# Three chained layers on one core: small layer-norm products inside attention's bursts, four PSUM buffers for the gated layer's first V tiles, output weights split later

## The chip, the core and the metric

The kernel runs on one core of a Trainium2 chip. The metric is the time of the whole program on the device in microseconds, the median of several runs. [...]

## What is computed

Attention over 8 heads in a window of 128 with a linear bias, then a two-matrix layer with a norm in front (the "first layer" below, 512 to 2048 to 512), then a gated layer with a mixing matrix over the 576 positions. Batch 4, model width 512, all in float32.

```python
attn = softmax(scale * q @ k.T + bias, masked to 0 <= rel < 128) @ v
x    = attn as (4, 576, 512)
xn   = (x - mean) / sqrt(var + 1e-6) * g_ln
x    = x + relu(xn @ w_ch1) @ w_ch2
h    = gelu(x @ w_in);  u, v = halves of h
v_n  = norm(v) * g_ln
v_s  = einsum('ts,bsd->btd', w_sg, v_n) + b_sg
out  = x + (u * v_s) @ w_out
```

## The kernel before

Matrix products of float32 accuracy are made of three products of rounded parts: a high part and a low part of each factor (names ending in h and l), without low times low. Splitting is work for the other engines: ScalarE writes the high part, GpSimd (POOL) or VectorE (DVE) the rest. The weight matrices come as 64-bit floats and are first turned to 32 bits by integer operations on VectorE (class Split64, lines 81, 83, 85 and 88), between two ScalarE operations (76 and 92); GpSimd then makes the low part (93).

Phase 1 holds attention and the first layer. Its order is made by a planner (class Sched): each generator yields operations with an engine, a planned duration, a priority, tokens it needs and buffers it takes; the planner always issues what can start first, and the program keeps that order on every engine. Positions are handled in nine groups g of 256 columns (two per batch, and group 8 for the last 64 positions of all batches). The first layer runs as a stream of pieces: m1 (line 785, into PSUM tile ps_h) and m2 (line 796, into PSUM tile acc), each piece 24 matmuls of 256 columns. From run KB = 13 on, attention's TensorE work comes in bursts between such pieces (function burst): scores of the next run (454, or 440 for the last 64 positions), value products of the run before (622, into PSUM tile o), transposes of this one (582, tps). PACE and BB set how early attention's units are due against the stream.

Each group's norm (functions norm, center, spread) needs three small products on TensorE: the mean (644 or 653), the sum of squares (701) and the spread of the reciprocal deviation over all partitions (711). Each is a planner operation of its own and takes one of the two ps_h buffers. For groups 3 to 8 GpSimd first adds the parts, so that one product is enough. The reciprocal deviation is applied only when a group's last m2 is evacuated (735, 739).

At the end of attention (end_attention) PSUM and SBUF space is released, and the generators flow (one per weight block) load and split the gated layer's weights: V half and U half of w_in (wv, wu), the first batch's x (x2), the mixing matrix (ws) and the output weights (wo, four blocks). Two V tiles of the gated layer (early_v) are planned around the last m2 piece, each 12 matmuls of 512 columns (line 1037) into one of two PSUM buffers ps_v.

Phase 2 (Phase2.run) is written in program order with chunks: v_tile (V: product, GELU, norm, split), u_chunk (U: 24 matmuls of 288 columns, GELU), vs_chunk (SG: mixing product of 28 matmuls, gate, split into gh and gl) and out_chunk (O). A V tile's GELU is Square and Tanh on ScalarE (1069, 1071) with VectorE between and behind (1070, 1074); then statistics (1088 to 1090), a power on GpSimd (1091), the norm (1094) and a split (1028, 1029). The parts of the fifth V tile are called vt. play() issues a chunk's matmuls, then one further step of each chunk that is pending, then some ticks; a tick loads and splits weights or the next batch's x. first_tail (971) splits the last 64 columns of the first batch's x2, which come from group 8 of the first layer; every U chunk reads them.

```python
# before, phase 2, first batch
play(V(0)[:2])
self.first_tail(x8)
...
play([V(0)[2], V(0)[3], U(0)[0], V(0)[4]] + U(0)[1:], 2)
self.need("ws")
```

Of the kernel before, what the change touches and what calls it, by code (L numbers as in the profile page):

```python
# [20 lines left out]
G = 2 * B + 1  # L21
# [24 lines left out]
LQ = 1, 0, 3, 2, 4, 8  # L46
EPRI = (-1, 9)

# [10 lines left out]
KB = 13  # L59
BB = 11, 6  # L60

# [160 lines left out]
def phase1(tc, nc, a, x2d, cst, p2):  # L222
# [361 lines left out]
    def burst(s):  # L584
        n = s.n
        after = runs[n + 1] if n + 1 < len(runs) else None
        nd = [("nm", e.un) for e in s.units] + [("bl", e.un - 2) for e in s.units if e.un - 2 < s.units[0].un]
        nd += [("R", n - 1), "cst", "unf"] + ([("A1", n)] if n == KB else [])
        sl = [("o", 1, ("ev", n - 1))]
        if after:  # L590
            nd += [("lq", n + 1), ("lk", n + 1)]
            sl.append(("s", 1, ("cp", n + 1)))
        dur = 300 + 140 * len(s.units) + (400 if runs[n - 1].tail else 820 if runs[n - 1].i0 else 600)
        if after:
            dur += 420 if after.tail else 850 if after.i0 else 600
# [6 lines left out]
        for z in [("A1", n + 1), ("C", n - 1)] + [("T", e.un) for e in s.units]:  # L602
            sched.done[z] = sched.free["PE"] + HOPP
# [27 lines left out]
    def gain(xh, xl, xc, p):  # L631
        act.activation(out=xh[:, p], in_=xc[:, p], func=ACTF.Copy, scale=g1[:, p:p + 1])
        dve.scalar_tensor_tensor(out=xl[:, p], in0=xc[:, p], scalar=g1[:, p:p + 1], in1=xh[:, p].bitcast(F32),
                                 op0=ALU.mult, op1=ALU.subtract)

    def norm(g):
        evs = [("ev", s.n) for s in runs if s.x() == g]
        pri = start[g] - LBACK[g == 8]
        last_m1 = ("m1", *[z for z in stream if z[0] == g][-1], 1)
        if g < NF:  # L640
            yield Op("PE", 1720, pri, need=evs, slots=[("h", 2, ("xc", g))])
            ps = ps_h.tile([128, 2, 256], F32, tag="h", name="ps_ln")
# [38 lines left out]
    def spread(g, xc, pri):  # L681
        pri += LQ[3]
        yield Op("ACT", 1040, pri, slots=[("ls", 2, ("var", g)), ("ls", 2, ("sq2", g))], token=("sq", g))
        sq = [ln_tile("sq") for z in range(2)]
# [3 lines left out]
        if g >= NF:  # L688
            yield Op("POOL", 1260, pri, token=("sq2", g))
            t = sq[0]  # L690
            pool.tensor_tensor(out=t, in0=sq[0], in1=sq[1], op=ALU.add)
            yield Op("POOL", 687, pri)
            pool.tensor_tensor(out=t[:, 0], in0=t[:, 0], in1=t[:, 1], op=ALU.add)
            parts = parts[:1]
        yield Op("PE", 230 * len(parts), pri + LQ[4], slots=[("h", 2, ("ve", g))], token=("var", g))
        if g < NF:
            sched.done["sq2", g] = sched.free["PE"] + HOP
        ps = ps_h.tile([128, 2, 256], F32, tag="h", name="ps_ln")
        for z in range(2):
            for x, t in enumerate(parts):  # L700
                pe.matmul(ps[:, 0, z:z + 1], t[:, 128 * z:128 * z + 128], ones[:, 0:1], start=x == 0,  # L701
                          stop=x + 1 == len(parts))
        yield Op("DVE", 70, pri + LQ[4], token=("ve", g), slots=[("vb", 2, ("rs0", g))])
# [3 lines left out]
        pool.tensor_tensor(out=v, in0=v, in1=mh.to_broadcast([128, 2]), op=ALU.pow)  # L707
        yield Op("PE", 430, pri + LQ[5], slots=[("h", 2, ("rstd", g))], token=("rs0", g))
        ps = ps_h.tile([128, 2, 256], F32, tag="h", name="ps_r")
        for z in range(2):  # L710
            pe.matmul(ps[:, 0, 128 * z:128 * z + 128], v[:, z:z + 1].to_broadcast([128, 128]), ident, start=True,
                      stop=True)
        yield Op("ACT", 275, pri + LQ[5], slots=[("rb", 3, ("x2", g))], token=("rstd", g))
# [191 lines left out]
class Phase2:  # L905
# [124 lines left out]

    def v_products(self, i):
# [9 lines left out]
    def early_v(self, i, pri):  # L1041

        yield Op("PE", 2560, pri, need=[("sc2", n) for n in range(4)] + [("st2", 8)])
        self.early[0, i] = self.v_products(i)

    def run(self, x8, left):
# [240 lines left out]
```

## Time and profile before

| | |
|---|---|
| median of 3 runs | 754.61 us (753.49 to 755.19) |
| profiled execution | 752.81 us, span 750.8 us |
| TensorE (PE) busy | 736.4 us, 98% of the span |
| VectorE, ScalarE, GpSimd busy | 60%, 41%, 33% |
| granted TensorE clock, mean | 0.995 |
| phase 1's last m2 matmul | about 533.4 us after the span's start |

PE's busy time is that of overlapping pipelined matmuls, so its share says that it was never long idle, not that it ran at its peak. The time between the starts of neighbouring rows tells how long a matmul held the engine. Times in rows are microseconds from the span's start.

### The profile page before, as it was taken

How to read it: one execution, taken by the hardware profiler on the slowest of the kernel's cores; microseconds unless marked ns; L12 is line 12 of the kernel's file. 1: busy time of each engine (PE TensorE's matmuls, PEld its weight loads, DVE VectorE, ACT ScalarE, POOL GpSimd, SP SyncE). 2: the span in 40 equal slices, each digit the busy share in tenths (PEclk: the TensorE clock that was granted, in tenths of full speed). 3: DMA queues.
4: the chain of work that ended last, by engine and by line, in shares of the span. 5: the costliest groups of instructions: out<-in, count | busy, mean ns of one | idle time of the engine just before them, and what ended most of it. 6: DMA issues, size and time to landing. Idle time of an engine off the chain costs nothing.

```text
span 750.8 us, 15850 instructions
## 1 busy us (share of the span) xinstructions
PE 736.4 (98%) x6270; PEld 685.9 (91%) x6270; DVE 448.3 (60%) x1149; ACT 308.5 (41%) x795; POOL 245.8 (33%) x307
## 2 busy tenths in 40 slices
PE   7999999999999999999999999999899999999998
PEld 3669899999999999999999999999799999999997
DVE  6899889896643453453343438434966746647632
ACT  5896755544323323433323424233453334243410
POOL 2533432333313212222212423026356307327220
PEclk9999999999999999999999999999999999999999
DMA  8654631331121020021122234304500050160002
GB/s 296 220 176 117 190 106 34 92 106 51 56 89 52 25 69 26 27 85 29 28 66 58 71 90 131 124 30 139 183 24 2 31 173 0 48 206 0 1 33 94
DMA packets 51625, 63.41 MB, mean 84 GB/s; under 512 B 10336, under 2 KB 38880, under 8 KB 51552
## 3 DMA queue, kind: packets, MB, share of 16 engines
q1 hardware_dynamic: 51552, 62.41, 26.5%
q8 instruction: 49, 0.80, 0.4%
q14 instruction: 24, 0.20, 0.1%
HBM read 52.96 MB, written 9.44 MB: 83 GB/s over the span
## 4 chain that ended last, share of the span: by engine, by line
PE 93%; DVE 2%; DMA 1%; ACT 1%; POOL 1%; issue 1%; SPq 0%; DVEq 0%; POOLq 0%; ACTq 0%
PE ps_h L785 26%; PE acc L796 25%; PE ps_s L1130 8%; PE ps_u L1113 7%; PE ps_o L1158 7%; PE ps_v L1037 6%; PE o L622 5%; PE tps L582 3%; PE s L454 3%; PE ps_ln L701 1%; DMA st<-in_w 1%; PE ps_ln L644 1%; DMA st<-in_wo 1%; PE ps_w L356 1%; PE s L440 1%
## 5 line engine op out<-in xcount | busy, mean ns | idle before, releaser
L796 PE MATMUL acc<-hh,w2h 128*128 128x256 f32 x576 | 163.6, 284 | 0.0
L785 PE MATMUL ps_h<-xh,w1h 128*128 128x256 f32 x576 | 163.0, 283 | 0.0
L785 PE MATMUL ps_h<-xl,w1h 128*128 128x256 f32 x576 | 160.2, 278 | 0.0
L785 PE MATMUL ps_h<-xh,w1l 128*128 128x256 f32 x576 | 160.1, 278 | 0.0
L796 PE MATMUL acc<-hl,w2h 128*128 128x256 f32 x576 | 160.1, 278 | 0.0
L796 PE MATMUL acc<-hh,w2l 128*128 128x256 f32 x576 | 160.0, 278 | 0.0
L726 DVE SCALAR_TENSOR_TENSOR hl<-ps_h,hh 128x512 fp32r<-128x512 f32 x72 | 49.7, 690 | 127.3 <-ACT hh L724 127.0
L785 PEld LDWEIGHTS ps_h<-xh,w1h 128*128 128x128 f32 x576 | 108.6, 188 | 1.0 <-issue 0.9
L796 PEld LDWEIGHTS acc<-hh,w2h 128*128 128x128 f32 x576 | 108.7, 189 | 0.7 <-DVE sc L85 0.3
L796 PEld LDWEIGHTS acc<-hl,w2h 128*128 128x128 f32 x576 | 108.4, 188 | 0.2
L785 PEld LDWEIGHTS ps_h<-xl,w1h 128*128 128x128 f32 x576 | 108.4, 188 | 0.1
L785 PEld LDWEIGHTS ps_h<-xh,w1l 128*128 128x128 f32 x576 | 108.3, 188 | 0.0
L796 PEld LDWEIGHTS acc<-hh,w2l 128*128 128x128 f32 x576 | 108.3, 188 | 0.0
L724 ACT ACTIVATE hh<-ps_h 128x512 fp32r<-128x512 f32 x72 | 42.8, 595 | 138.8 <-PE ps_h L785 138.8
L463 POOL TENSOR_SCALAR_AFFINE_SELECT m<-m 128x256 f32<-128x256 f32 x100 | 44.7, 452 | 143.7 <-ACT m L543 141.6
L505 ACT ACTIVATE t<-t,sm 128x128 f32<-128x128 f32 x144 | 56.1, 394 | 14.6 <-DVE sm L499 14.6
L513 POOL TENSOR_TENSOR t<-t,sm 128x256 f32<-128x256 f32 x52 | 32.9, 633 | 42.4 <-DVE sm L509 34.9
L76 ACT ACTIVATE sc<-st 128x512 f32<-128x512 f32 (+1 forms) x52 | 30.9, 599 | 24.6 <-DMA st<-in_w 6.7
L1029 POOL TENSOR_TENSOR gl<-gt,gh 128x576 fp32r<-128x576 f32 x16 | 22.9, 1429 | 53.0 <-ACT gh L1028 53.0
L1071 ACT ACTIVATE ge<-ge 128x512 f32<-128x512 f32 (+1 forms) x34 | 22.4, 657 | 34.9 <-DVE ge L1070 34.9
L85 DVE SCALAR_TENSOR_TENSOR sc<-st,sc 128x512 int32<-128x512 int32 (+1 forms) x52 | 35.9, 692 | 0.3
L622 PE MATMUL o<-m,rv 128*64 128x128 f32 (+3 forms) x416 | 34.7, 296 | 0.3 <-POOL m L463 0.3
(163 smaller groups left out, 1530.5 us busy)
## 6 DMA issues: line engine op xcount, KB each, us to landing
st<-in_w SPq DMA_DIRECT2D x24, 512.0 KB, 4.2
x2d<-x SPq DMA_DIRECT2D x18, 256.0 KB, 2.0
out<-xr SPq DMA_DIRECT2D x15, 288.0 KB, 2.1
st<-in_w SPq DMA_DIRECT2D x16, 256.0 KB, 2.6
st<-in_wi SPq DMA_DIRECT2D x8, 512.0 KB, 3.9
st<-x2d SPq DMA_DIRECT2D x8, 512.0 KB, 5.1
xr<-x2d SPq DMA_DIRECT2D x8, 512.0 KB, 6.3
rq<-in_q SPq DMA_DIRECT2D x28, 128.0 KB, 3.2
```

Of the source, the lines that this page charges most:

```text
L85: dve.scalar_tensor_tensor(out=xi, in0=self.wh, scalar=-0x40000000, in1=xi, op0=ALU.bitwise_and, op1=ALU.bitwise_or)
L463: pool.affine_select(out=out, in_=in_, pattern=pat, compare_op=ALU.is_ge, fill=0.0, base=-1 if up else 0, channel_multiplier=1 if up else -1)
L505: act.activation(out=t[:, h], in_=t[:, h], func=ACTF.Exp, bias=st[:, h:h + 1], scale=-1.0, accum_out=sums[:, h, 0:1])
L622: pe.matmul(s.O[64 * h:64 * h + 64, oc:oc + w], v, s.M[m][0:k, h, mc:mc + w], start=x == 0, stop=x == len(mm) - 1, skip_group_check=True)
L724: act.activation(out=h, in_=ps, func=ACTF.Relu)
L726: dve.scalar_tensor_tensor(out=l, in0=ps, scalar=0.0, in1=h.bitcast(F32), op0=ALU.max, op1=ALU.subtract)
L785: pe.matmul(ps[:, half], w[:, kc, f], m[:, kc], start=kc == 0 and x == 0, stop=kc == 3 and x == 2)
L796: pe.matmul(accs[half][:, d], w[:, f, ds], m[:, k], start=fi and d == 0 and k == 0 and x == 0, stop=la and k == 1 and x == 2, skip_group_c ...
L1037: self.nc.tensor.matmul(ps, xs[s][:, kc, c0:c0 + 128], self.wv[m][:, kc], start=kc == 0 and x == 0, stop=kc == 3 and x == 2)
L1113: pe.matmul(ps[:, z, 0:288], wu[s][:, kc, ds], self.x[m][:, kc, 288 * z:288 * z + 288], start=kc == 0 and x == 0, stop=kc == 3 and x == 2)
L1130: pe.matmul(ps[:, z, 0:288], l, r[:, 288 * z:288 * z + 288], start=n == 0, stop=n == len(mm) - 1)
L1158: pe.matmul(ps[:, z, 0:288], wo[s][:, kc, ds], gated[b][m][:, kc, 288 * z:288 * z + 288], start=n == 0, stop=n == 11)
```

## The change

It has three parts.

1. For groups 3 to 7 the three small products are no longer planner operations of their own. They are put on a list (riders), and the next burst whose needs are met issues them between its value products and its transposes. Their results go to the second half of attention's PSUM tile o (ob[:, 256:512]), not to a ps_h buffer. GpSimd's last addition goes to a buffer of its own (rd). BB's first number moves attention two units ahead.
2. A PSUM pool ps_e with two buffers is opened at the end of attention beside ps_v. Four V tiles are planned early, one ahead of the last m2 piece and three behind it; V tiles 0 and 1 use ps_e. The pool ps_u of phase 2 is opened only after these four tiles have been played, without ticks, and first_tail comes after them. The order after that is U, U, V tile 4, U, U.
3. The output weights (wo) are not split by flow; they remain queued for the ticks of phase 2.

```diff
-EPRI = (-1, 9)
+EPRI = (-1, 9, 10, 11)
-BB = 11, 6
+BB = 13, 6
@@ burst
         values(runs[n - 1])
+        ride = [r for r in riders if all(sched.done.get(z, 1e9) <= sched.now for z in r[0])]
+        for r in ride:
+            riders.remove(r)
+            r[1]()
+            sched.free["PE"] += r[2]
         for e in s.units:
             transposed(e)
@@ new functions
+    def products(g, fn, dur, pri, free, token):
+
+        if g < NF or g == G - 1:
+            yield Op("PE", dur, pri, slots=[("h", 2, free)], token=token)
+            ps = ps_h.tile([128, 2, 256], F32, tag="h", name="ps_ln")
+            fn(ps)
+            return ps
+        ps = ob[:, 256:512].rearrange("p (o c) -> p o c", o=1)
+        yield Op(None, 0, pri, token=("ride", *token))
+        riders.append(((("ride", *token), ("rstd", g - 1)), lambda: fn(ps), dur, token))
+        yield Op(None, 0, pri, need=[token])
+        return ps
+
+    def last_sum(g, t, token, pri):
+
+        y = t[:, 0]
+        yield Op("POOL", 687, pri, slots=[] if g == G - 1 else [("rd", 1, token)], token=("rd", *token))
+        if g < G - 1:
+            y = P["st"].tile([128, 256], F32, tag="rd", name="rd", bufs=1)
+        pool.tensor_tensor(out=y, in0=t[:, 0], in1=t[:, 1], op=ALU.add)
+        return y
@@ norm (spread is changed alike for its two products)
-            yield Op("PE", 427, pri + LQ[1], slots=[("h", 2, ("xc", g))], token=("mean", g))
-            ps = ps_h.tile([128, 2, 256], F32, tag="h", name="ps_ln")
-            pe.matmul(ps[:, 0], ones, t[:, 0], start=True, stop=True)
+            y = yield from last_sum(g, t, ("mean", g), pri)
+            parts = [y]
+
+        def mean(ps):
+            for x, y in enumerate(parts):
+                pe.matmul(ps[:, 0], ones, y, start=x == 0, stop=x + 1 == len(parts), skip_group_check=True)
+
+        ps = yield from products(g, mean, 430 * len(parts), pri + LQ[1] * (g >= NF), ("xc", g), ("mean", g))
@@ end_attention
+        p2.ps_e = tc.alloc_tile_pool(name="ps_e", bufs=2, space=PSUM, side="right", reuse_waits="tile")
-        for n, j in enumerate(list(p2.queue)):
+        for n, j in enumerate(z for z in list(p2.queue) if z.name != "wo"):
             sched.spawn(p2.flow(sched, j, n), sched.now)
-        for i in range(2):
+        for i in range(4):
             sched.spawn(p2.early_v(i, when[2, stream[-1]] + EPRI[i]), sched.now)
@@ v_products
-        ps = self.ps_v.tile([128, DG], F32, tag="v", name="ps_v")
+        ps = (self.ps_e if b == 0 and i < 2 else self.ps_v).tile([128, DG], F32, tag="v", name="ps_v")
@@ Phase2.run
-        play(V(0)[:2])
+        play(V(0)[:4], 0)
+        self.ps_e.release()
+        ps_u = tc.alloc_tile_pool(name="ps_u", bufs=3, space=PSUM, reuse_waits="tile")
         self.first_tail(x8)
...
-        play([V(0)[2], V(0)[3], U(0)[0], V(0)[4]] + U(0)[1:], 2)
+        play(U(0)[:2] + V(0)[4:] + U(0)[2:], 2)
```

TensorE, the sum of squares of group 3 in the first layer. Before, in the middle of an m1 piece:

```order
L785 MATMUL ps_h_2934<-xh_1475,w1h3_2039 128x256
L785 MATMUL ps_h_2934<-xl_1476,w1h3_2039 128x256
L785 MATMUL ps_h_2934<-xh_1475,w1l3_2040 128x256
L701 MATMUL ps_ln_2953<-ones_73,sq_2857 128x1 x2
L785 MATMUL ps_h_2934<-xh_1475,w1h3_2039 128x256
L785 MATMUL ps_h_2934<-xl_1476,w1h3_2039 128x256
```

In the change (line numbers shift; 818 is m1, 627 the value products, 728 the squares):

```order
L818 MATMUL ps_h_3060<-xh_2807,w1l0_95 128x256
L454 MATMUL s_150<-rk_2531,rq_2526 64x64 x2
L454 MATMUL s_150<-rk_2531,rq_2526 64x128 x2
L454 MATMUL s_150<-rk_2531,rq_2526 64x192 x4
L627 MATMUL o_146<-m_2749,rv_2294 64x256 x2
L627 MATMUL o_146<-m_2752,rv_2294 64x128 x2
L728 MATMUL o_146<-ones_73,rd_2844 128x1 x2
L582 MATMUL tps_142<-ident_71,t_2760 128x128 x2
L582 MATMUL tps_142<-ident_71,t_2803 128x128 x2
L818 MATMUL ps_h_3060<-xh_2807,w1h0_94 128x256
```

The two products left the m1 piece for a burst that was there anyway; the same holds for the other 14.

ScalarE at the start of the gated layer (ge is the GELU's tile: Square reads ps_v, Tanh reads ge; x2h of x and xth of x are first_tail). Before:

```order
L1069 ACTIVATE ge_7106<-ps_v_7014 128x512
L1071 ACTIVATE ge_7106<-ge_7106 128x512
L1069 ACTIVATE ge_7113<-ps_v_7065 128x512
L1071 ACTIVATE ge_7113<-ge_7113 128x512
L92 ACTIVATE woh_6935<-sc_7028 128x512
L1028 ACTIVATE x2h_6665<-x_5432 128x4x64
L1028 ACTIVATE xth_6937<-x_5432 128x512
L1028 ACTIVATE vnh_7095<-vg_7107 128x512
```

In the change:

```order
L1105 ACTIVATE ge_7073<-ge_7073 128x512
L1063 ACTIVATE vnh_7059<-vg_7068 128x512
L1103 ACTIVATE ge_7098<-ps_v_7085 128x512
L1105 ACTIVATE ge_7098<-ge_7098 128x512
L1063 ACTIVATE vnh_7059<-vg_7074 128x512
L1103 ACTIVATE ge_7126<-ps_v_7113 128x512
L1105 ACTIVATE ge_7126<-ge_7126 128x512
L1063 ACTIVATE x2h_6666<-x_5325 128x4x64
L1063 ACTIVATE xth_6934<-x_5325 128x512
```

The split of the last columns stood behind two V tiles' Tanh and now stands behind four.

ScalarE in the mixing stage of batch 0 (x2h of st is the split of batch 1's x). Before:

```order
L1071 ACTIVATE ge_7353<-ge_7353 128x576
L1028 ACTIVATE gh_7358<-gt_7389 128x576
L1028 ACTIVATE x2h_6665<-st_7393 128x4x256
L1028 ACTIVATE gh_7358<-gt_7426 128x576
L1028 ACTIVATE x2h_6665<-st_7395 128x4x256
```

In the change, where L1168 and L1171 on VectorE make gt:

```order
L92 ACTIVATE woh_6932<-sc_7263 128x512
L76 ACTIVATE sc_7349<-st_7238 128x512
L92 ACTIVATE woh_6932<-sc_7306 128x512
L1063 ACTIVATE gh_7351<-gt_7382 128x576
L92 ACTIVATE woh_6932<-sc_7349 128x512
L1063 ACTIVATE x2h_6666<-st_7389 128x4x256
L1063 ACTIVATE gh_7351<-gt_7425 128x576
```

The split of batch 1's x now stands behind the fourth output-weight block, whose last VectorE operation stands behind the gate of the second SG chunk:

```order
L1168 SCALAR_TENSOR_TENSOR gt_7425<-ps_s_7396,g2_6798,bb_6797 128x576
L1171 TENSOR_TENSOR gt_7425<-gt_7425,u_7158 128x576
L88 SCALAR_TENSOR_TENSOR sc_7349<-st_7238,sc_7349 128x512
```

Before, no output-weight operation stood in this stage on VectorE.

## Rows read from the trace of the kernel before

**Rows 1.** The page's part 4, the chain that ended last: share of the span by engine.
```profile
PE 93%; DVE 2%; DMA 1%; ACT 1%; POOL 1%; issue 1%; SPq 0%; DVEq 0%; POOLq 0%; ACTq 0%
```

**Rows 2.** TensorE's timeline behind group 3's sum of squares: start, us, instruction.
```profile
200.92 0.36 PE L785 MATMUL ps_h<-xh,w1h 128*128 128x256 f32 x1
201.12 0.28 PE L785 MATMUL ps_h<-xl,w1h 128*128 128x256 f32 x1
```

**Rows 3.** The chain in order of time, two pieces of the stream: start, us, what.
```profile
196.47 2.83 PE acc L796 x24
...
226.87 2.72 PE ps_h L785 x24
```

**Rows 4.** TensorE's timeline, first matmuls of V tiles 1 and 2, U, V tile 4.
```profile
533.50 0.39 PE L1037 MATMUL ps_v<-wvh,x2h 128*128 128x512 f32 x1
...
539.68 0.50 PE L1037 MATMUL ps_v<-wvh,x2h 128*128 128x512 f32 x1 [3.25 <-DVE vg L1074]
...
546.89 0.42 PE L1113 MATMUL ps_u<-x2h,wuh 128*128 128x288 f32 x2
...
550.08 0.40 PE L1037 MATMUL ps_v<-wvh,xth 128*128 128x512 f32 x1
```

**Rows 5.** Windows: us, busy PE PEld DVE ACT POOL, granted clock, DMA share, GB/s.
```profile
540.40:544.00 3.60, 3.60 (x11) 2.79 (x10) 3.19 (x8) 2.50 (x5) 1.94 (x3) 0.53 1.10 389
```

**Rows 6.** The chain in order of time, four SG chunks and two V tiles.
```profile
562.63 14.93 PE ps_s L1130 x112
577.56 5.45 PE ps_v L1037 x24
```

**Rows 7.** VectorE's timeline: last evacuations (L735), GELU and statistics of V tile 1.
```profile
533.54 0.68 DVE L735 TENSOR_TENSOR et<-acc,rstd 128x512 f32<-128x512 f32 x1
...
534.87 0.69 DVE L735 TENSOR_TENSOR et<-acc,rstd 128x512 f32<-128x512 f32 x1
...
540.68 0.68 DVE L1070 SCALAR_TENSOR_TENSOR ge<-ge,ps_v 128x512 f32<-128x512 f32 x1
...
543.72 0.16 DVE L1090 TENSOR_SCALAR ba<-ba 128x1 f32<-128x1 f32 x1
```

**Rows 8.** ScalarE's timeline: Tanh of V tile 1, output weights, first_tail.
```profile
541.39 0.63 ACT L1071 ACTIVATE ge<-ge 128x512 f32<-128x512 f32 x1 [2.22 <-DVE ge L1070]
541.92 0.61 ACT L92 ACTIVATE woh<-sc 128x512 fp32r<-128x512 f32 x1
542.45 0.40 ACT L1028 ACTIVATE x2h<-x 128x256 fp32r<-128x256 f32 x1
```

**Rows 9.** GpSimd's timeline: output weights, first_tail, vt, batch 1's x.
```profile
528.02 1.30 POOL L93 TENSOR_TENSOR wol<-sc,woh 128x512 fp32r<-128x512 f32 x1 [3.64 <-ACT woh L92]
...
543.86 0.74 POOL L1029 TENSOR_TENSOR x2l<-x,x2h 128x256 fp32r<-128x256 f32 x1
...
560.88 2.65 POOL L1029 TENSOR_TENSOR vt<-vg,vt 64x512 fp32r<-64x512 f32 x2 [1.33 <-ACT vt L1028]
...
570.42 2.38 POOL L1029 TENSOR_TENSOR x2l<-st,x2h 128x1024 fp32r<-128x1024 f32 x1
```

**Rows 10.** VectorE's timeline: output weights (L83, L85), U's GELU, gates (L1134, L1137).
```profile
524.97 0.43 DVE L83 TENSOR_SCALAR sc<-sc 128x512 int32<-128x512 int32 x1
525.44 0.69 DVE L85 SCALAR_TENSOR_TENSOR sc<-st,sc 128x512 int32<-128x512 int32 x1
...
528.37 1.49 DVE L85 SCALAR_TENSOR_TENSOR sc<-st,sc 128x512 int32<-128x512 int32 x1
...
552.99 0.74 DVE L1070 SCALAR_TENSOR_TENSOR ge<-ge,ps_u 128x576 f32<-128x576 f32 x1
...
566.52 0.81 DVE L1134 SCALAR_TENSOR_TENSOR gt<-ps_s,g,bb 128x576 f32<-128x576 f32 x1
567.37 0.76 DVE L1137 TENSOR_TENSOR gt<-gt,u 128x576 f32<-128x576 f32 x1
...
570.99 2.44 DVE L1137 TENSOR_TENSOR gt<-gt,u 128x576 f32<-128x576 f32 x1
```

More of the change, by code (lines that the diff above doesn't have):

```diff
@@ L599, in burst @@
         values(runs[n - 1])
+        ride = [r for r in riders if all(sched.done.get(z, 1e9) <= sched.now for z in r[0])]
[3 more added lines that the diff above has]
+            sched.free["PE"] += r[2]
         for e in s.units:
             transposed(e)
-        for z in [("A1", n + 1), ("C", n - 1)] + [("T", e.un) for e in s.units]:
+        for z in [r[3] for r in ride] + [("A1", n + 1), ("C", n - 1)] + [("T", e.un) for e in s.units]:
             sched.done[z] = sched.free["PE"] + HOPP
@@ L634, in gain @@
                                  op0=ALU.mult, op1=ALU.subtract)
+    riders = []
+    def products(g, fn, dur, pri, free, token):
[16 more added lines that the diff above has]
+        return y
     def norm(g):
@@ L640, in norm @@
         if g < NF:
-            yield Op("PE", 1720, pri, need=evs, slots=[("h", 2, ("xc", g))])
-            ps = ps_h.tile([128, 2, 256], F32, tag="h", name="ps_ln")
-            for p in range(4):
-                pe.matmul(ps[:, 0], ones, xt[g][:, p], start=p == 0, stop=p == 3)
+            yield Op(None, 0, pri, need=evs)
+            parts = [xt[g][:, p] for p in range(4)]
         else:
-            yield Op("POOL", 1260, pri, need=evs, slots=[("ls", 2, ("mean", g))])
+            yield Op("POOL", 1260, pri, need=evs, slots=[("ls", 2, ("mean", g) if g == G - 1 else ("rd", "mean", g))])
             t = ln_tile("sum")
             pool.tensor_tensor(out=t, in0=xt[g][:, 0:2], in1=xt[g][:, 2:4], op=ALU.add)
-            yield Op("POOL", 687, pri)
-            pool.tensor_tensor(out=t[:, 0], in0=t[:, 0], in1=t[:, 1], op=ALU.add)
-            yield Op("PE", 427, pri + LQ[1], slots=[("h", 2, ("xc", g))], token=("mean", g))
-            ps = ps_h.tile([128, 2, 256], F32, tag="h", name="ps_ln")
-            pe.matmul(ps[:, 0], ones, t[:, 0], start=True, stop=True)
+            y = yield from last_sum(g, t, ("mean", g), pri)
[4 more added lines that the diff above has]
+        ps = yield from products(g, mean, 430 * len(parts), pri + LQ[1] * (g >= NF), ("xc", g), ("mean", g))
         yield Op("DVE", 1210, pri + LQ[1], need=["al2"], slots=[("xcb", 1, ("xhl", g))], token=("xc", g))
@@ L691, in spread, with squares @@
             pool.tensor_tensor(out=t, in0=sq[0], in1=sq[1], op=ALU.add)
[L692 to L695, printed above, removed]
+            parts[:] = [(yield from last_sum(g, t, ("var", g), pri))]
+        def squares(ps):
+            for z in range(2):
+                for x, t in enumerate(parts):
+                    pe.matmul(ps[:, 0, z:z + 1], t[:, 128 * z:128 * z + 128], ones[:, 0:1], start=x == 0,
+                              stop=x + 1 == len(parts), skip_group_check=True)
+        ps = yield from products(g, squares, 230 * len(parts), pri + LQ[4], ("ve", g), ("var", g))
         if g < NF:
             sched.done["sq2", g] = sched.free["PE"] + HOP
[L698 to L702, printed above, removed]
         yield Op("DVE", 70, pri + LQ[4], token=("ve", g), slots=[("vb", 2, ("rs0", g))])
@@ L707, in spread, with spread_out @@
         pool.tensor_tensor(out=v, in0=v, in1=mh.to_broadcast([128, 2]), op=ALU.pow)
[L708 to L712, printed above, removed]
+        def spread_out(ps):
+            for z in range(2):
+                pe.matmul(ps[:, 0, 128 * z:128 * z + 128], v[:, z:z + 1].to_broadcast([128, 128]), ident, start=True,
+                          stop=True, skip_group_check=True)
+        ps = yield from products(g, spread_out, 430, pri + LQ[5], ("rstd", g), ("rs0", g))
         yield Op("ACT", 275, pri + LQ[5], slots=[("rb", 3, ("x2", g))], token=("rstd", g))
@@ L843, in end_attention @@
     def end_attention():
-        yield Op(None, 0, 0, need=[("ev", s.n) for s in runs] + [("w", n) for n in range(40)], token="attention")
+        yield Op(None, 0, 0, need=[("ev", s.n) for s in runs] + [("w", n) for n in range(40)] + [("rstd", G - 2)],
+                 token="attention")
         for p in (P["st"], raw, ap2, ps_s, ps_o, ps_t):
@@ L1078, in v_tile @@
         def v_tile(b, i):
-            ps = self.early.pop((b, i)) if (b, i) in self.early else self.v_products(i)
+            ps = self.early.pop((b, i)) if (b, i) in self.early else self.v_products(b, i)
             first, last = gelu2(ps, [DG])
```

10 lines of the change are left out of this document (5 added, 5 removed).

## The prediction

> **What bounds the kernel now.** I read the chain of waits first: 93% of the span is TensorE work [rows 1], so a change counts only where it shortens TensorE's own stream or makes TensorE wait. Then TensorE's timeline, for the two places that the change edits.
>
> In the first layer TensorE never waits: its rows follow each other without an idle mark. What can be won there is friction. After a solitary norm product the first matmul holds TensorE for 0.20 us, 200.92 to 201.12 [rows 2]; an ordinary one holds it 0.113 us, 2.72 over 24 [rows 3]. There are also two paces: some pieces of 24 run in 2.72 us, others in 2.83 [rows 3], or 4.6 ns per matmul. Going through the timeline break by break, the slow pace always follows a mean or a squares product; after bursts of six value products it is nearly always fast, after bursts of four it is either.
>
> At the start of the gated layer stands the one long wait. V tile 1 starts at 533.50 and should hand over some 2.73 us later (24 V matmuls take 5.45 [rows 6]), at 536.23; V tile 2 starts at 539.68, after 3.25 us of idle ended by VectorE's GELU of tile 0 freeing a PSUM buffer [rows 4]. [...] So this place costs 3.4 us of waiting and 1.76 us of slow clock.
>
> **Part 1, small products in bursts.** Three products of each of five norms, 15 in all, move behind the value products of a burst. They are the same products, so their own time moves along and I count it as zero. Removed are 15 returns to the stream at 0.20 - 0.113 = 0.09 us [rows 2, 3]: -1.35 us. A burst pays its own return once, as now. Bounds: 0 (the rider pays the same inside the burst) to -2.7 (entering cost as much as leaving). I take -1.35, the end that a row shows.
>
> [...]
>
> The pace: after solitary products of these norms I count eleven slow stretches with 432 matmuls, the first at 189.8 and the last at 431.1 us, so 432 x 4.6 ns = 2.0 us; after bursts another 1.6 us. In the change each such stretch hangs on a burst. If half of them turn fast: -1.0 us. Bounds: all 1920 matmuls of these five blocks slow, 8.8 against 3.6 us now, is +5.2; all fast is -3.6.
>
> The longer latency of a norm (mean, squares and spread now wait a burst each) costs nothing: the gain is applied only when a block ends, and BB starts attention two units earlier. If that cover failed, m1 of the next block would wait for xh and xl.
>
> **Part 2, four PSUM buffers.** The wait at 536.23 goes: V tiles 1 to 3 run from 533.50 to 533.50 + 3 x 2.73 = 541.7. What is late next? The first U product needs the last 64 columns of x2, which first_tail splits, and ScalarE's queue now has that split behind the Tanh of V tile 3. On VectorE the last evacuation can start once the first half of acc is complete, about 532.4 (before it started at 533.54 [rows 7], held up by output-weight splitting). Four operations follow; two take 534.87 - 533.54 = 1.33 us [rows 7], so the GELU of V tile 0 starts at 532.4 + 2.66 = 535.05. One V tile occupies VectorE from the GELU at 540.68 to past 543.72 [rows 7], 3.1 us with the hand-over. Tile 3's GELU: 535.05 + 3 x 3.1 = 544.4. Its Tanh follows 0.71 later (540.68 to 541.39), the next ScalarE instruction 0.53 after that, and x2h takes 0.40 [rows 7, 8]: 546.05. GpSimd's x2l takes 0.74 [rows 9]: 546.85. The fourth matmul of U needs it. So TensorE idles from 541.7 to about 546.8 but for a few matmuls, longer than today. U's remaining 21 of 24 matmuls take 2.8 us (3.19 from 546.89 to 550.08 [rows 4]) and the slow clock again costs 1.76: U ends at 551.4 instead of 550.08. The same five chunks are then done, so this part costs **+1.3 us**, not -5. Bounds: -0.5 if the clock is not lowered this time, +2.5 if VectorE's pitch is 0.4 us longer per tile. Even with VectorE free, tile 3 ends at 541.7 and its GELU, Tanh and x2l still follow, so the gap cannot close.
>
> **Part 3, output weights split later.** Today all four splits start beside the last work of the first layer. Now they enter VectorE, ScalarE and GpSimd between the U and SG chunks. One costs VectorE two operations of 0.43 and two of 0.69, then ScalarE 0.61 (woh) and GpSimd 1.30 (wol) [rows 8 to 10]. The third VectorE operation of the next split waits while GpSimd runs: L85 took 1.49 instead of 0.69 just as wol ran at 528.02 [rows 9, 10]. Following the queues from U's end at 551.4 (U 3.19, V 2.73, SG 3.73 = 14.93/4 [rows 6]):
> - U 1 ends 554.6, V tile 4 557.35, U 2 560.55, U 3 563.75. V tile 4's GELU starts about 558.2; behind it stand three operations of split 1, GELU and statistics, U 2's GELU (0.74), the last of split 1 (to 563.6). Then woh to 564.2, wol to 565.5, the blocked operation of split 2 to 566.2, V tile 4's norm to 566.7. ScalarE and GpSimd make vt: half of 2.65 [rows 9] plus a ScalarE operation like woh, 568.7. SG 0 needs vt for its last four of 28 matmuls, at 563.75 + 3.2 = 566.95: **wait 1.75**.
> - SG 0 then ends at 569.2, SG 1 at 573.0. VectorE has U 3's GELU, splits 2 and 3 and gate 0 (0.81 and 0.76 [rows 10]) before gate 1, which starts about 578 instead of 573. Split 4's last operation stands behind gate 1, ScalarE's woh behind that, and batch 1's x2h behind that: 581.7. GpSimd's x2l (2.38 [rows 9]) is done at 584.4, or a gate product later. TensorE is through with SG 3 at 580.6 and needs x2h at once and x2l two matmuls later: **wait 3.3 to 4.9**.
> Sum 5.0 to 6.7; with 0.2 for a U buffer that comes free late I take **+6.0**. Bounds: 0 (the backlog is covered; today x2l is ready at 572.8, 4.7 us before V(1) starts [rows 6, 9]) to +8.2 (every gate product takes the 2.44 us that one took while GpSimd ran [rows 10]).
>
> A gap of some 4 us before V(1) should lower the clock again, as after 3.25 us today: **+1.76** [rows 4, 5], bounds 0 and 1.76.
>
> **Sum.** The profiled execution took 752.81 us, 1.80 below the median of the runs, 754.61. -1.35 - 1.0 + 1.3 + 6.0 + 1.76 = +6.7: 759.5 on that execution, **761.3 us** on the median.
>
> **Rivals.**
> 1. Not slower: the output splits find room in the U and SG stage, so x2l of batch 1 is complete before SG 3 ends (about 579). Part 3 and the second slow clock are then 0: 754.61 - 1.35 - 1.0 + 1.3 = 753.6. For it: TensorE has no wait in this stage today, and x2l has 4.7 us to spare. Against it: the split of batch 1 stands behind the fourth output split in two queues, which order alone fixes. It decides at a VectorE backlog under some 2 us at gate 1. With all bursts fast as well (-3.6): 751.0.
> 2. Breaks save nothing: behind the riders TensorE needs the same 0.09 us each that it needs today behind a solitary product, and all else stays: 761.3 + 1.35 = 762.7. For it: the riders keep full-array shape among half-array matmuls. Against it: the stream gets 15 returns fewer. [...]
> 3. Riders leave TensorE at the slow pace after every burst: 761.3 + 1.0 + 5.2 = 767.5. For it: every mean and squares product is followed by the slow pace today. Against it: in a burst the transposes come last.
> 4. The wait is removed as meant and nothing takes its place: 754.61 - 5.2 - 2.35 = 747.1 with part 3 hidden. The queue order of part 2 excludes it; I give it 0.02.
>
> **Chances.** A difference under 0.2% (1.5 us) is what a measurement of this kernel cannot tell from none. Forecast 0.65, rival 2 0.10, rival 3 0.05, rival 1 at 753.6 0.12 and with fast bursts 0.06, rival 4 0.02. Slower by over 0.2%: 0.65 + 0.10 + 0.05 = 0.80; same 0.12; faster 0.08. The forecast's own bounds, 756 to 766, hold rival 2; reaching down to 754.5 takes in half of rival 1: 754.5 to 766.
>
> **What would show it.** Right: V tiles 1 to 3 without a wait; then idle of some 4 to 5 us before U with ScalarE's x2h and GpSimd's x2l as releasers and a granted clock near 0.5 behind it; waits on vt in SG 0 and on x2h and x2l of batch 1 before V(1). Part 1 is right if stretches of the first layer lose the 0.20 us returns and its end comes about 2 us earlier. Wrong: U following V tile 3 within 2 us, or V(1) following SG 3 at once.

## The result and the profile after

The changed kernel takes 764.3 us (763.89 to 765.63, 4 runs) against 754.73 us before: a ratio of 1.0132, interval 1.0115 to 1.0150. The forecast was 761.3 in a range of 754.5 to 766.0. Direction and range held; the size, +6.7, came out as +9.6.

The profiled execution took 763.89 us, its span is 762.1. The chain of waits, which was 93% TensorE [rows 1], in the page of the changed kernel:

```profile
PE 91%; DVE 4%; ACT 2%; POOL 2%; issue 1%; DVEq 0%; POOLq 0%; ACTq 0%
```

TensorE's waits in the changed kernel, in the view of waits (engine, tile and line waiting, who ended it: us in total, times, longest):

```profile
PE ps_u L1147 <- ACT x2h L1063: 4.1, 1, 4.1
...
PE ps_v L1072 <- POOL x2l L1064: 2.5, 1, 2.5
PE ps_s L1164 <- POOL vt L1064: 1.5, 1, 1.5
...
PE ps_v L1072 <- ACT x2h L1063: 1.0, 1, 1.0
PE ps_s L1164 <- DVE u L1108: 0.8, 1, 0.8
```

The one long wait on VectorE's vg [rows 4] is gone. Five others stand in its place, on the tiles that the prediction names: x2h in U 0, vt in SG 0, a U buffer (ahead of SG 2), and batch 1's x2h and x2l at the start of V(1), the V stage of batch 1. On TensorE's timeline the longest of them look like this:

```profile
542.98 0.29 PE L1147 MATMUL ps_u<-x2h,wuh 128*128 128x288 f32 x1
547.35 0.61 PE L1147 MATMUL ps_u<-x2h,wuh 128*128 128x288 f32 x1 [4.08 <-ACT x2h L1063]
...
583.53 0.50 PE L1072 MATMUL ps_v<-wvh,x2h 128*128 128x512 f32 x1 [1.05 <-ACT x2h L1063]
583.87 0.40 PE L1072 MATMUL ps_v<-wvl,x2h 128*128 128x512 f32 x1
586.76 0.79 PE L1072 MATMUL ps_v<-wvh,x2l 128*128 128x512 f32 x1 [2.50 <-POOL x2l L1064]
```

The granted clock, a share of full speed, falls behind both long waits, to 0.57 from 547 to 551 us and to 0.50 from 586 to 590, as it fell to 0.53 at one place before [rows 5]. Windows of the changed kernel (columns as there):

```profile
547.00:549.00 2.00, 1.65 (x5) 1.34 (x6) 1.74 (x5) 1.34 (x3) 1.62 (x2) 0.58 0.14 57
549.00:551.00 2.00, 2.00 (x11) 2.00 (x10) 0.00 (x0) 0.00 (x0) 2.00 (x3) 0.57 0.03 8
551.00:553.00 2.00, 2.00 (x17) 2.00 (x16) 0.00 (x0) 0.54 (x1) 0.10 (x1) 1.00 0.00 0
...
588.00:590.00 2.00, 2.00 (x6) 1.51 (x6) 0.00 (x0) 0.04 (x1) 2.00 (x2) 0.50 0.00 0
590.00:592.00 2.00, 2.00 (x7) 1.56 (x6) 0.00 (x0) 0.57 (x1) 2.00 (x2) 0.58 0.00 0
```

Where the time went, from the starts of TensorE's matmuls in the two traces. Each line is a stretch between two marks that both kernels have.

| stretch | before | after | difference | predicted |
|---|---|---|---|---|
| span's start to the first m1 matmul | 51.94 | 52.05 | +0.11 | 0 |
| first m1 matmul to V tile 0 | 475.98 | 477.13 | +1.15 | -2.35 |
| V tile 0 to the end of four V tiles, the last m2 piece and U 0 | 22.16 | 23.02 | +0.86 | +1.3 |
| from there to the end of SG 3 | 27.32 | 30.13 | +2.81 | +1.95 |
| waits ahead of and in V(1) | 0 | 3.85 | +3.85 | +4.05 |
| V(1) tiles 0 and 1 without these waits | 5.45 | 8.00 | +2.55 | +1.76 |
| from there to the last matmul | 163.90 | 163.90 | 0 | 0 |

The sum is +11.3 us, the difference of the two spans. It comes from one execution of each kernel. The two profiled executions are 1.9 and 0.4 below their medians, so the medians differ by less, 9.6.

### The profile page after: what moved, and what is told of

The parts are those of the page before. It is cut to its first block, busy times and chain, and to the rows that moved or that the text cites. A ratio compares the mean times of both kernels' runs of the same rounds, so it can differ in the third digit from the quotient of the medians.

```text
span 762.1 us, 15834 instructions
## 1 busy us (share of the span) xinstructions
PE 740.9 (97%) x6270; PEld 688.8 (90%) x6270; DVE 444.3 (58%) x1149; ACT 311.3 (41%) x803; POOL 244.7 (32%) x302
## 4 chain that ended last, share of the span: by engine, by line
PE 91%; DVE 4%; ACT 2%; POOL 2%; issue 1%; DVEq 0%; POOLq 0%; ACTq 0%
PE ps_h L818 26%; PE acc L829 26%; PE ps_o L1192 7%; PE ps_u L1147 6%; PE ps_s L1164 6%; PE ps_v L1072 5%; PE o L627 4%; PE s L454 3%; PE tps L582 3%; PE ps_ln L681 1%; PE ps_ln L728 1%; PE ps_w L356 1%; DVE sc L85 1%; DVE ge L1104 1%; PE s L440 1%
## 5 line engine op out<-in xcount | busy, mean ns | idle before, releaser
L463 POOL TENSOR_SCALAR_AFFINE_SELECT m<-m 128x256 f32<-128x256 f32 x96 | 42.5, 446 | 130.8 <-ACT m L543 128.2
L513 POOL TENSOR_TENSOR t<-t,sm 128x256 f32<-128x256 f32 x47 | 29.6, 630 | 45.1 <-DVE sm L509 30.5
L85 DVE SCALAR_TENSOR_TENSOR sc<-st,sc 128x512 int32<-128x512 int32 (+1 forms) x52 | 38.9, 750 | 0.3
```

Of the source, the lines that this page charges most:

```text
L85: dve.scalar_tensor_tensor(out=xi, in0=self.wh, scalar=-0x40000000, in1=xi, op0=ALU.bitwise_and, op1=ALU.bitwise_or)
L463: pool.affine_select(out=out, in_=in_, pattern=pat, compare_op=ALU.is_ge, fill=0.0, base=-1 if up else 0, channel_multiplier=1 if up else -1)
```

## The experiments

Two lengths compare the kernels better than their whole times, since they leave the start out: from the first m1 matmul to V tile 0 ("stream"), and from there to the start of the last matmul ("rest"). All from the traces, in us. "Whole" is the median, or the one time of a run that was not repeated.

| kernel | stream | rest | whole | ratio, interval |
|---|---|---|---|---|
| before | 475.98 | 218.83 | 754.7 | |
| the change | 477.13 | 228.91 | 764.3 | 1.0132, 1.0115 to 1.0150 |
| e1, riders alone | 477.04 | 219.94 | 754.93 | 1.0018, 1.0008 to 1.0029 |
| e2, four buffers alone | 476.07 | 222.55 | 757.19 | 1.0057, 1.0030 to 1.0084 |
| e3, weights late alone | 476.08 | 225.01 | 759.39 | 1.0084, 1.0066 to 1.0101 |
| e4, four buffers, first_tail early | 476.08 | 215.45 | 749.93 | 0.9954, 0.9939 to 0.9969 |
| e5, e4 with V tile 4 sooner | 475.98 | 215.39 | 749.85 | 0.9950, 0.9933 to 0.9967 |
| e6, the change, first_tail early | 477.17 | 223.39 | 759.13 | one run |
| e7, the change, x ahead of weights | 477.13 | 232.90 | 768.03 | one run |
| e8, riders behind the transposes | 475.18 | 218.90 | 752.64 | one run |
| e9, e8 and e4 together | 475.18 | 215.58 | 751.14 | 0.9965, 0.9953 to 0.9976 |
| e10, BB = 13 alone | 476.26 | 218.99 | 753.92 | one run |
| e11, the change without wol | 477.04 | 225.25 | 760.53 | one run |

The medians of before in these comparisons lie between 753.26 and 753.86, while the expectations reckon from 754.7, so a whole time falls 0.9 to 1.5 us lower in its range for this alone. The stream's length repeats within 0.15 us among kernels whose small products stand alike, so 1 us there is far above its scatter. The rest is less sure: it holds what the lowered clock cost in the one execution that was traced, and behind equal waits that cost differed by up to 1.2 us (last section).

**e1, part 1 alone.** The change with parts 2 and 3 undone; against before, besides products, last_sum, norm and spread as in the change:

```diff
-BB = 11, 6
+BB = 13, 6
...
+        for r in ride:
+            riders.remove(r)
+            r[1]()
+            sched.free["PE"] += r[2]
         for e in s.units:
             transposed(e)
```

> Part 1 alone (riders and BB = 13), the other two undone. Theory A, riders save nothing: in the changed kernel V tile 0 starts 1.27 us later than before (529.19 against 527.92), and burst by burst a rider adds 0.37 to 0.55 us where a solitary product adds 0.43 to 0.46; then the same 1.3 us are lost here, about 756.0 against 754.7, and V tile 0 starts near 529.2. Theory B, the riders win 2.35 us as I predicted and the loss of phase 1 comes from the other two parts (the splits that no longer run beside its end): 752.4, V tile 0 near 525.6.

Theory A: the stream is 1.06 us longer than before, as in the whole change. The rest is also 1.11 longer; the wait ahead of V tile 2 is 3.57 instead of 3.25 [rows 4], and V tiles 2 and 3 take 8.00 instead of 7.21 behind it. These two make up the 1.11: 0.32 of waiting, and 0.79 because the granted clock over the two tiles is 0.67 here and 0.76 before. e8, with the same riders one place later, and e10, with BB alone, show 0.76 there and a rest within 0.16 us of before, so the 0.79 is not shown to be the riders'. The mean granted clock of e1's ten runs lies between 0.991, as in the traced one, and 0.995; their ratio, 1.0018, is some 1.4 us, not the 2.2 of the trace.

**e2, part 2 alone.** The change with part 1 undone, and part 3:

```diff
-        for n, j in enumerate(z for z in list(p2.queue) if z.name != "wo"):
+        for n, j in enumerate(list(p2.queue)):
```

> Part 2 alone: four early V tiles in four PSUM buffers, first_tail behind them, output weights split where they were before. Theory A, the wait moves to the split of the last 64 columns, which stands behind the fourth Tanh on ScalarE: V tiles 1 to 3 without a wait, then 4 to 6 us of idle ended by ScalarE's x2h, longer by up to 2 us than in the changed kernel because the output-weight splits share VectorE; 755.6 to 758.2. Theory B, four buffers close the gap and all the loss is the output weights': 754.7 - 5.0 = 749.7.

Theory A, with a wait half a microsecond longer than it allowed. Four buffers by themselves lose 3.7 us of rest. ScalarE's timeline of e2 shows the split directly behind the fourth Tanh, and the view of TensorE's waits what that costs:

```profile
548.15 0.63 ACT L1071 ACTIVATE ge<-ge 128x512 f32<-128x512 f32 x1 [1.32 <-DVE ge L1070]
548.69 0.40 ACT L1029 ACTIVATE x2h<-x 128x256 fp32r<-128x256 f32 x1
```
```profile
PE ps_u L1113 <- ACT x2h L1029: 6.5, 1, 6.5
```

The wait is 2.5 us longer than in the change, since here the output-weight splits share VectorE with the four GELUs.

**e3, part 3 alone.**

```diff
-        for n, j in enumerate(list(p2.queue)):
+        for n, j in enumerate(z for z in list(p2.queue) if z.name != "wo"):
```

> Part 3 alone: output weights split by the ticks of phase 2, two PSUM buffers as before. Theory A, this part costs waits in the mixing stage and before V(1), with a lowered clock behind the long one, whatever the V tiles do: 4 to 9 us of TensorE waits between 555 and 590, 760 to 764. Theory B, the backlog needs the four early V tiles (U 0 and U 1 late, V tile 4 behind U 1) and alone it is covered: 754 to 755, the wait before V tile 2 shorter by up to 1 us since VectorE evacuates the last acc sooner.

Both halves of the expectations have a part in it. The backlog costs its waits without part 2, as theory A has it: one wait of 7.7 us for a U buffer, and the clock at 0.52 behind it. Theory B's side remark holds too, and by more than the 1 us it gave: the wait ahead of V tile 2 falls from 3.25 to 0.7, and V tiles 2 and 3 take 5.98 instead of 7.21 us. The whole lies at 759.39, a little under A's 760 to 764; this helps, and so does the lower median of before beside it, 753.26. TensorE's waits, VectorE's timeline and a window of e3:

```profile
PE ps_s L1130 <- DVE u L1074: 7.7, 1, 7.7
PE ps_v L1037 <- DVE vg L1074: 0.7, 1, 0.7
```
```profile
562.31 0.68 DVE L88 SCALAR_TENSOR_TENSOR sc<-st,sc 128x512 int32<-128x512 int32 x1
562.91 0.42 DVE L81 TENSOR_SCALAR sc<-sc 128x512 f32<-128x512 f32 x1
563.37 0.43 DVE L83 TENSOR_SCALAR sc<-sc 128x512 int32<-128x512 int32 x1
563.83 1.72 DVE L85 SCALAR_TENSOR_TENSOR sc<-st,sc 128x512 int32<-128x512 int32 x1
565.47 0.53 DVE L1094 TENSOR_SCALAR vg<-vg,ba 128x512 f32<-128x512 f32 x1
565.92 0.74 DVE L1074 SCALAR_TENSOR_TENSOR u<-ge,ps_u 128x576 f32<-128x576 f32 x1
```
```profile
566.50:571.50 5.00, 4.69 (x20) 4.72 (x21) 3.07 (x5) 3.30 (x6) 3.26 (x3) 0.52 0.01 3
```

Four operations of weight splits stand ahead of the operation that frees U's buffer at 566.66, and TensorE starts SG at 566.81.

**e4, four buffers with first_tail early.** Part 2 alone, and:

```diff
-        play(V(0)[:4], 0)
-        self.ps_e.release()
-        ps_u = tc.alloc_tile_pool(name="ps_u", bufs=3, space=PSUM, reuse_waits="tile")
+        play(V(0)[:1], 0)
         self.first_tail(x8)
+        play(V(0)[1:4], 0)
+        self.ps_e.release()
+        ps_u = tc.alloc_tile_pool(name="ps_u", bufs=3, space=PSUM, reuse_waits="tile")
```

> Part 2 alone with one move more: first_tail right behind the first V tile's Tanh instead of behind the fourth's. Theory A, the queue order makes the wait: no idle before U, no lowered clock there, 5.0 us less than before and about 1 us of a new wait for vt in the first mixing product: 749.7 to 751.5. Theory B, VectorE is the bound of this stretch whatever the order (four GELUs at 3.1 us each): U then waits for a PSUM buffer or the mixing stage for vt as long as x2l was waited for, 754 or more.

Theory A, with its number: 3.4 us less rest than before, and the only cost is the new wait of 1.55 us for vt. TensorE goes from V tile 3 to U without a mark, and comes to wait in SG 0. TensorE's and GpSimd's timelines of e4:

```profile
541.32 0.39 PE L1038 MATMUL ps_v<-wvh,x2l 128*128 128x512 f32 x1
541.54 0.42 PE L1113 MATMUL ps_u<-x2h,wuh 128*128 128x288 f32 x2
...
562.02 0.53 PE L1130 MATMUL ps_s<-wsh,vt 128*128 128x288 f32 x2 [1.55 <-POOL vt L1030]
```
```profile
539.20 0.75 POOL L1030 TENSOR_TENSOR x2l<-x,x2h 128x256 fp32r<-128x256 f32 x1 [0.57 <-ACT x2h L1029]
```

x2l is done at 539.95, 1.6 us before U's first matmul. One place in a queue made the difference between +3.7 (e2) and -3.4 us. It beats both kernels.

**e5, V tile 4 sooner.**

```diff
-        play(U(0)[:2] + V(0)[4:] + U(0)[2:], 2)
+        play(U(0)[:1] + V(0)[4:] + U(0)[1:], 2)
```

> The kernel of run e4_buffers_split_early with V tile 4 behind U 0 instead of behind U 1, as the kernel before has it. Theory A, VectorE takes V tile 4's GELU one chunk sooner and the wait of 1.55 us for vt in the first mixing product goes, against 0.5 to 1.1 us of waits for a PSUM buffer: 749.0 to 749.9. Theory B, V tile 4 needs V tile 2's buffer, which VectorE frees late, and waits longer than vt did: 750.5 or more.

Inside the range of A, but nothing is gained on e4: the wait for vt goes, and 1.17 us for V tile 2's buffer come in its place.

**e6, the whole change with first_tail early** (the change, with the edit of e4).

> The whole change with one move: first_tail right behind the first V tile's Tanh. Theory A, two separate causes: the gap before U (4.4 us and the lowered clock behind it, about 1.3 us) goes, while the output weights' waits stay, some of them 1 to 2 us longer because U comes sooner: 758 to 761. Theory B, VectorE's backlog sets the end of this stage, so what is won before U is waited for in the mixing stage: 763 to 764.5, waits there longer by 4 us.

Theory A: 5.5 us less rest than the change. The gap ahead of U is gone, the weights' waits stay: 2.8 us for vt instead of 1.5, and 0.5 and 2.5 us ahead of V(1).

**e7, x ahead of the weights.**

```diff
-        self.w_jobs("wo", self.a["wo"])
...
             self.tail_jobs(nb)
+            if b == 0:
+                self.w_jobs("wo", self.a["wo"])
             play(SG(b), 2)
```

> The whole change, but the output weights enter the queue of the ticks behind batch 1's x instead of ahead of it. Theory A, the three engines are short of time in this stage whatever the order: no wait for vt and none before V(1), but the output products of batch 0 then wait for woh and wol, 6 us or more: 762 to 768. Theory B, only the order is bad: the 3.84 us before V(1) and the 2.55 us of lowered clock behind it go and nothing comes in their place: 755 to 758.

Theory A. The waits for vt and for batch 1's x are gone, and TensorE waits for the weights and the gates in the output products instead, 7.0 us in sum, with a granted clock of 0.50 from 589.5 to 602.5; 4.0 us more rest than the change. The whole, 768.03, stands at the very end of A's range. TensorE's waits of e7:

```profile
PE ps_o L1191 <- ACT woh L92: 3.4, 3, 1.4
PE ps_o L1191 <- ACT gh L1062: 1.7, 1, 1.7
PE ps_o L1191 <- POOL gl L1063: 1.3, 1, 1.3
...
PE ps_o L1191 <- POOL wol L93: 0.6, 1, 0.6
```

So this other order of the same work does not save part 3. A third order was not tried.

**e8, riders behind the transposes.** Part 1 alone with the loop over riders moved:

```diff
-        for r in ride:
-            riders.remove(r)
-            r[1]()
-            sched.free["PE"] += r[2]
         for e in s.units:
             transposed(e)
+        for r in ride:
+            riders.remove(r)
+            r[1]()
+            sched.free["PE"] += r[2]
```

> Part 1 alone with the riders behind the transposes, the last thing in the burst. The stretch from the first m1 matmul to V tile 0 took 475.98 to 476.08 us in four kernels without riders and 477.04 to 477.13 in two with them. Theory A, a product costs its own 0.45 us wherever it stands, and a solitary one costs nothing beside: 475.9 to 477.2. Theory B, the place between value products and transposes is at fault, a change of tile shape more per rider: behind the transposes the saving of 1.35 us and more shows, 474.7 or less.

The number, 475.18, lies between the two expectations: 0.8 under before, far from the 1.35 and more of theory B. Two things add up in it. What the products and their breaks take falls by 0.17 us against before; the other 0.63 is the pace (below). Against e1 the place in the burst is worth 0.05 us for each mean or spread product, nothing for a squares product. TensorE's timeline of the same burst with a spread product, e1 and then e8:

```profile
221.05 0.87 PE L627 MATMUL o<-m,rv 128*64 128x256 f32 x8
221.85 0.71 PE L742 MATMUL o<-ident,var 128*128 128x128 f32 x4
222.40 0.60 PE L582 MATMUL tps<-ident,t 128*128 128x128 f32 x4
222.75 0.36 PE L818 MATMUL ps_h<-xh,w1h 128*128 128x256 f32 x1
```
```profile
221.85 0.66 PE L582 MATMUL tps<-ident,t 128*128 128x128 f32 x4
222.34 0.61 PE L742 MATMUL o<-ident,var 128*128 128x128 f32 x4
222.71 0.36 PE L818 MATMUL ps_h<-xh,w1h 128*128 128x256 f32 x1
```

Behind the values the four products take 0.55 us (221.85 to 222.40) and the transposes 0.35; with the transposes first these take 0.49 and the products 0.37. The stream returns after 0.90 and after 0.86 us.

**e9, the edits of e8 and e4 together**, output weights where they were before.

> The change mended by what the runs so far showed: riders behind the transposes (e8), four buffers with first_tail behind the first Tanh (e4), output weights split where they were before. Theory A, the gains add: 0.8 us of the stream (475.98 to 475.18) and 3.4 us after V tile 0 (218.83 to 215.45): 4.2 us, ratio 0.9944. Theory B, the shifted attention (BB) changes where the weight splits fall beside the last piece, as in e1, where the part behind V tile 0 became 1.1 us longer: 0.9955 or more.

In the trace theory A holds: stream 475.18, rest 215.58, 4.05 us less than before in sum. The whole times give 0.9965, which is not better than e4, outside A's 0.9944 and within the number of theory B, though the longer rest that B gives as its reason is not there. The start ahead of the first m1 matmul took 52.92 us in this trace, 51.94 before, 51.68 in e4; it varied from 51.68 to 52.92 over the profiled kernels, with no cause shown. What follows the start of the last matmul took 4.30 us here, 4.01 before. Why the whole times win less than the two lengths stays open. e4 and e5 have the lowest medians measured; their intervals overlap with that of e9.

**e10, attention two units ahead alone.**

```diff
-BB = 11, 6
+BB = 13, 6
```

> The kernel before with BB = 13 alone, every small product solitary. Theory A, BB shifts only where bursts stand: first m1 to V tile 0 in 475.8 to 476.3 us, so the difference of e1 and e8 (477.04 and 475.18) is the riders'. Theory B, the pace depends on where bursts stand in the pieces, and BB alone makes it 0.7 us longer or shorter.

Theory A: 476.26, within the range given. Against it, with the same BB, riders behind the values lose 0.78 us of stream (e1) and riders behind the transposes win 1.08 (e8): the 1.86 between those two is the riders' place.

**e11, the change without GpSimd's low parts of the output weights.** Left out is wol, set to zero once, so the products with it add nothing.

```diff
         self.nc.scalar.activation(out=h, in_=self.x, func=ACTF.Copy)
+        if l is None:
+            return
```

> The whole change without GpSimd's four low parts of the output weights (wol is set to zero once, early; so the low-part terms of the output product are left out). Theory A, VectorE's operations that stood still beside them (1.75 us instead of 0.69, three times) and GpSimd's 1.3 us each make the backlog: vt 1 us earlier, the gates on time, the wait before V(1) down from 3.84 to some 2 us, 758 to 761. Theory B, VectorE's and ScalarE's own operations fill their queues anyway: the waits change by under 1 us in all, 763 to 764.

Theory A: 3.7 us less rest. The three operations that took 1.75 to 1.83 us beside wol (L85; 1.49 in [rows 10]) fall to 0.69, and the waits shrink, the one for vt from 1.5 to 0.4, the one for x2l from 2.5 to 1.7; those for a U buffer and for batch 1's x2h go. The run takes away GpSimd's four operations and VectorE's standing still at once and does not tell their shares. VectorE's and GpSimd's timelines of the change, then VectorE's of e11:

```profile
565.13 1.76 DVE L85 SCALAR_TENSOR_TENSOR sc<-st,sc 128x512 int32<-128x512 int32 x1
```
```profile
565.04 1.30 POOL L93 TENSOR_TENSOR wol<-sc,woh 128x512 fp32r<-128x512 f32 x1 [1.33 <-ACT woh L92]
```
```profile
566.66 0.69 DVE L85 SCALAR_TENSOR_TENSOR sc<-st,sc 128x512 int32<-128x512 int32 x1
```

L85, which reads st and sc, took 1.76 us beside wol in the change and 0.69 without it in e11. What in the two engines makes it stand still is not shown.

## Why the prediction was right in sign and short in size

**The breaks, -1.35: wrong, measured +0.3.** The failed step is "Removed are 15 returns to the stream at 0.20 - 0.113 = 0.09 us". I read only the far end of a break. TensorE's timeline of before around it, whose next two rows are those of [rows 2]:

```profile
200.43 0.28 PE L785 MATMUL ps_h<-xh,w1l 128*128 128x256 f32 x1
200.55 0.50 PE L701 MATMUL ps_ln<-ones,sq 128*128 128x1 f32 x4
```

From 200.43 to 201.12 lie one m1 matmul, four product matmuls and the returning matmul: six in 0.69 us, 0.115 each. The four hold the engine for only 0.37 us (200.55 to 200.92), 0.09 less than four such slots, and the return's extra 0.09 only makes that up. This solitary product costs four slots of the stream and nothing beside, so it paid no return that could be removed. Measured break by break (from the last stream matmul's start to the second one behind, less two slots of 0.113), a solitary mean, squares or spread product costs 0.44, 0.46 and 0.46 us. A rider adds, to a burst of eight value products of 2.21 us in e1:

| | mean | squares | spread |
|---|---|---|---|
| behind the values (e1) | +0.37 | +0.34 | +0.49 |
| behind the transposes (e8) | +0.32 | +0.34 | +0.45 |

and to one of twelve value products (2.36 us on average) 0.55, 0.52 and 0.45 in e1. Over all 15 that makes 6.9 us, against 6.8 for as many solitary ones. All breaks of the stream together take 81.4 us in the change and 81.1 before. My rival 2 ("breaks save nothing", chance 0.10) had the size of this term; its reason, a return paid again behind each rider, is not what the rows show.

The trace of before held this answer. Only 14 of the 15 products were solitary; the sum of squares of group 7 stood at the end of a burst already:

```profile
421.29 0.28 PE L785 MATMUL ps_h<-xh,w1l 128*128 128x256 f32 x1
...
423.01 0.51 PE L701 MATMUL ps_ln<-ones,sq 128*128 128x1 f32 x4
...
423.58 0.28 PE L785 MATMUL ps_h<-xl,w1h 128*128 128x256 f32 x1
```

This break costs 2.07 us by the same measure; the bursts of the same make around it, without a norm product, cost 1.62 and 1.63. So the product costs 0.45 in a burst, as much as a solitary one.

**The pace, -1.0: wrong in sign.** Above 113.3 ns per matmul the stream lost 5.82 us before, 6.65 in the change, 6.56 in e1, but 5.19 in e8 and 5.91 in e10. I took half of the stretches behind riders to be fast. Of the 15 stretches behind a rider 10 are slow throughout in the change, and 7 in e8. The stretches are also longer, since no solitary product ends them any more: behind the 15 products stood 504 matmuls before, 432 of them in slow stretches, and stand 1332 in the change, 756 of them in stretches that are slow throughout. I kept the 432. My rival 3 (all slow, +5.2) was too much, my forecast too little. What sets the pace is not settled: the 15 stretches come out alike in all five traces with riders behind the values, but in e8 bursts of the same make are followed by either pace, and no run here takes it apart.

**Part 2, +1.3: right in each step,** measured +0.86. Shifted by the 1.27 us by which V tile 0 was late, VectorE's GELU of tile 0 was predicted at 536.32 and stands at 536.30; its pitch was predicted as 3.1 and is 3.12 (539.42, 542.54, 545.65); the end of x2l was predicted at 548.12 and is 548.11. ScalarE's and GpSimd's timelines:

```profile
546.36 0.63 ACT L1105 ACTIVATE ge<-ge 128x512 f32<-128x512 f32 x1 [1.28 <-DVE ge L1104]
546.90 0.40 ACT L1063 ACTIVATE x2h<-x 128x256 fp32r<-128x256 f32 x1
```
```profile
547.38 0.73 POOL L1064 TENSOR_TENSOR x2l<-x,x2h 128x256 fp32r<-128x256 f32 x1 [0.92 <-ACT x2h L1063]
```

Only the clock behind it cost less: twenty U matmuls from 548.57 to 552.21 took 3.64 instead of 2.66 us, 1.0 where I had put 1.76. The 1.76 is what V tiles 2 and 3 took before, 546.89 - 539.68 = 7.21 us [rows 4], less the 5.45 of [rows 6], at a granted clock of 0.53 from 540.4 to 544.0 [rows 5]. In e11, behind the same wait of 4.08 us, the last 23 matmuls of U 0 took 6.01 instead of 4.85, so that this term came out below the forecast and not above it is luck. "Even with VectorE free ... the gap cannot close" was true of this order and false of the program: e4 closes it.

**Part 3, +6.0: right in mechanism,** measured 2.81 + 3.85 = 6.66. The chain of the split of batch 1 is the predicted one: the fourth split's last operation behind gate 1, woh behind that, x2h behind woh, x2l behind that. VectorE, ScalarE and GpSimd in the change:

```profile
580.12 1.15 DVE L1171 TENSOR_TENSOR gt<-gt,u 128x576 f32<-128x576 f32 x1
581.19 0.68 DVE L88 SCALAR_TENSOR_TENSOR sc<-st,sc 128x512 int32<-128x512 int32 x1
```
```profile
581.90 0.63 ACT L92 ACTIVATE woh<-sc 128x512 fp32r<-128x512 f32 x1 [3.89 <-DVE sc L88]
582.44 1.04 ACT L1063 ACTIVATE x2h<-st 128x1024 fp32r<-128x1024 f32 x1
```
```profile
583.84 2.86 POOL L1064 TENSOR_TENSOR x2l<-st,x2h 128x1024 fp32r<-128x1024 f32 x1
```

The wait for vt is 1.52 against 1.75, the one for a U buffer 0.82 against 0.2. Rival 1 (covered, 753.6) needed a backlog of under 2 us at gate 1: that gate, put at about 578 instead of 573, started at 579.28.

**The second slow clock, +1.76: right, undersized in this trace.** It took 2.55 us, 2.36 of them in eleven V matmuls, 586.76 to 591.62, which held TensorE for 4.86 us instead of 11 x 5.45 / 24 = 2.50 [rows 6]. In e6, behind a wait for x2l of the same 2.50 us, the last 22 matmuls of these two tiles took 6.73 instead of 7.43 us, 5.00 at the full clock: 1.73, about what I had put.

So of the 4.6 us between the forecast sum (+6.7) and the spans (+11.3), part 1 is 3.5: 1.7 from reading one end of a break, 1.8 from the pace. That the range held all the same is in part luck: part 1 came out with the wrong sign, and the range reached 4.7 us above the forecast.

## What to carry to other kernels

Price a small instruction inside a stream by the starts on both sides of it: time from the last stream instruction to the second one behind, less their own slots; a slow return alone proves nothing. When a buffer is added to remove a wait, list what the freed engine needs next and where its producer stands in its queue; here moving one split from behind the fourth Tanh to behind the first turned +3.7 into -3.4 us. Work moved from beside a long stream into a stage where three engines share short chunks was paid there, in both orders that were tried.

## What the runs showed of the hardware

- A norm product of one column took about as long in the stream as a matmul of 256 columns: 0.115 us on average of the six in the rows above, 0.113 for an ordinary one [rows 3]. A solitary product of one column (squares) and one of 128 columns (spread) both cost 0.46 us for four matmuls. In a burst the four of the squares added 0.34 to 0.52 us in e1. In the trace of before the four weight loads for the squares of group 3 start from 200.43 on and the next load at 200.89, 0.115 us each; whether the load is what holds such a product is not shown.
- A product right behind value products (e1) was a little dearer than one right behind transposes (e8): 0.05 us for mean and spread products, nothing for squares, in bursts of eight value products.
- The granted clock was lowered behind the wait of 1.71 us in V(1) in e11 (0.72 from 584 to 590), and not behind those of 1.55 us in e4 (1.00 from 562 to 568) and 1.66 us in e9 (1.00 from 562.4 to 568.4). What decides between them is not shown. In e11 the 22 V matmuls behind the wait took 6.73 us instead of 22 x 5.45 / 24 = 5.00 [rows 6], so that wait cost 1.7 us more than its own length.
- What the lowered clock costs behind a wait differs between traces: behind 4.08 us of waiting 23 U matmuls took 4.85 us in the change and 6.01 in e11, and behind 2.50 us 22 V matmuls took 7.43 in the change and 6.73 in e6. Whether the kernel or the execution makes the difference is not shown.
